# Two weight groups of a fused attention and MLP kernel loaded as one pair of 1024-column row blocks

## The chip, the cores and the metric

The kernel runs on one core of a Trainium2 chip. The metric is the device time of one launch in microseconds (us). A core has a matrix engine (TensorE, in profiles PE, with its weight loads as PEld), three engines for elementwise work (VectorE or DVE, ScalarE or ACT, GpSimd or POOL), and a queue engine (SyncE or SP) that issues most of the transfers between DRAM and the on-chip memory SBUF. Matmuls write to PSUM, which has eight banks here, PS0 to PS7, each 128 partitions by 512 float32.

## The reference

```python
def _attn_ref(q, k, v):                       # 8 batches, 8 heads, 576 tokens, 64 wide
    q_s = np.exp(q - np.max(q, axis=-1, keepdims=True))
    q_s = q_s / (np.sum(q_s, axis=-1, keepdims=True) + 1e-09)
    k_s = np.exp(k - np.max(k, axis=2, keepdims=True))
    k_s = k_s / (np.sum(k_s, axis=2, keepdims=True) + 1e-09)
    kv = np.einsum('bhsd,bhse->bhde', k_s, v)
    return np.einsum('bhsd,bhde->bhse', q_s, kv)

def _moe_ref(x, w_in, w_out, beta):           # x: 4608 x 512, w_in: 512 x 2048, w_out: 2048 x 512
    h = x @ w_in
    g = h * (1.0 / (1.0 + np.exp(-beta * h)))
    return g @ w_out
```

The attention result, with the heads side by side, is the x of the second function. Inputs and the output are float32.

## The kernel before

**Tiling.** The 4608 tokens are worked on in nine slabs of 512: the first 512 tokens of each of the eight batches, and a ninth slab of the 64 left over in each. A slab has a pass 1 (h for 16 tiles of 128 features, f = 0 to 15, each summed over four blocks m = 0 to 3 of the 512 inputs) and a pass 2 (four output tiles u = 0 to 3, each summed over the 16 features tiles). Between them ScalarE reads a finished h tile from its PSUM bank, applies the activation with beta, and writes it to GT in bfloat16 (L646). The attention of the next batch is mixed into the passes.

**Order.** The program is written out as one list of operations, each with its engine, the keys that it reads and writes, and the PSUM banks that it touches. The waits between engines are derived from that. Within an engine the order of the list is the order of execution; an instruction that waits holds up all that stand behind it on its engine. All transfers issued by SP move along one queue. In slab 0 the callbacks in the list `todo` put attention work of batch 1 between the matmuls of pass 2 at counted places.

**Weights.** w_in is loaded in float32 and cast to bfloat16 (`WIN`) in four groups c of 512 columns, that is, four feature tiles each: `load_win` (L565) issues the transfers, `cast_win` (L570, its instruction on L571) the casts. Each group has a staging buffer of [128, 4, 512] float32: WST0, WST1, and then the two output buffers O2S1 and O2S0, which are free at the start. Groups 0 to 2 come as four transfers of 256 KB (one block m each, rows of 2 KB), group 3 as two of 512 KB (two blocks m each, rows of 2 KB). After the casts, the same buffers take w_out (`load_wout`, L548), in pieces of 1 MB for f = 0 to 3, 4 to 7 and 8 to 11, then of 512 KB for 12 and 13, and of 256 KB each for 14 and 15. `scale_wout` (L558, its instruction on L560) multiplies each by 1/beta on VectorE and writes `WOUT` in bfloat16. Later O2S0 and O2S1 hold the finished output tiles for the stores.

**Slab 0.** `by_m(0, a, b)` gives a function that, for one m, runs the matmuls of tiles a to b - 1. The loop on L682 works through the groups of tiles 4 to 7, 8 to 11, 12 to 13 and 14 to 15, each over all four m. Which bank a tile of slab 0 uses is in `HFIRST` (L650): tiles 8 to 15 use banks 3, 4, 5, 6, 0, 1, 7, 2, and tiles 0 to 7 the same ones. Pass 2 of slab 0 writes its four outputs to banks 3, 4, 5 and 6, all four side by side for one f after the other:

```python
pass2_group(0, (0, 1, 2, 3), (3, 4, 5, 6), tick)
```

The work of batch 1 that stands around it in the list, before that call, is this. SP issues the loads for f = 0 and 4, the queries' first half, f = 8, the second half, then keys and values mixed with the remaining w_out loads. ScalarE takes the exponential of the queries (L312) after the last activation of pass 1, which needs a table load. `norm_main` then sums on VectorE (L336), takes the reciprocal there (L337) and multiplies on GpSimd (L338) for head pairs 0, 1, 3 and 2:

```python
scale_wout(0)
scale_wout(4)
exp_q(1, (0, 1, 3, 2))
norm_main(1, 0, 1, POOL)
scale_wout(8)
norm_main(1, 1, 1, POOL)
norm_main(1, 3, 1, POOL)
exp_kc(1, 0, 2)
scale_wout(12, 2)
cast_v(1, 1)
norm_main(1, 2, 1, POOL)
```

`scale_wout(14, 2)` and TensorE's transposes of the normalized queries of head pairs 0 and 1 (L368) follow as callbacks in pass 2.

Of the kernel before, what the change touches and what calls it, by code (L numbers as in the profile page):

```python
# [5 lines left out]
F32 = mybir.dt.float32  # L6
# [10 lines left out]
DM = H * D  # L17
DFF = 2048
NF = DFF // 128
NM = DM // 128  # L20
# [9 lines left out]
PE, ACTE, DVE, POOL, SP = "tensor", "scalar", "vector", "gpsimd", "sync"  # L30
# [13 lines left out]
class Program:  # L44
# [12 lines left out]
    def add(self, eng, fn, r=(), w=(), bank=(), slot=None, after=()):  # L57
        op = Op(eng, fn, slot)
        op.pos = len(self.ops)
        deps = op.deps  # L60
        deps.extend(after)
        for k in r:
            deps.extend(self.writer.get(k, ()))
            self.readers.setdefault(k, []).append(op)
        for k in w:
            for d in self.readers.get(k, ()):
                if d is not op and not self._same(d, op):
                    deps.append(d)
            for d in self.writer.get(k, ()):
                if not self._same(d, op):  # L70
                    deps.append(d)
            self.readers[k] = []
            self.writer[k] = [op]
        for k in bank:
            t = self.touch.setdefault(k, {})
            for e, d in t.items():
                if e != eng:
                    deps.append(d)
            t[eng] = op
        if eng == POOL and slot is None:  # L80
            if self.pool is not None:
                deps.append(self.pool)
            self.pool = op
        self.ops.append(op)
        return op
# [78 lines left out]
def bass_efficient_attn_shen__then__act_swish_beta_kernel(  # L164
# [10 lines left out]
    win_h, wout_h, beta_h, out_h = moe_w_in.tensor, moe_w_out.tensor, moe_beta.tensor, out.tensor  # L175

    with ExitStack() as es:
        def sb(name, shape, dt):
            return es.enter_context(nc.sbuf_tensor(name, shape, dt))
# [22 lines left out]
        WIN = sb("WIN", [128, NM, DFF], BF16)  # L202
        WST = [sb(f"WST{i}", [128, 4, DM], F32) for i in range(2)]
        WOUT = sb("WOUT", [128, NF, DM], BF16)
        GT = sb("GT", [128, NF, SM], BF16)
        O2S = [sb(f"O2S{i}", [128, 4, DM], F32) for i in range(2)]
        BT = sb("BT", [4, 512], F32)
        BC = sb("BC", [128, NF], F32)
        BETA = sb("BETA", [128, NF], F32)
        RB = sb("RB", [128, NF], F32)  # L210
# [12 lines left out]
        add = P.add  # L223
# [7 lines left out]
            r=["iota"], w=["idb"])  # L231
        add(POOL, lambda e: e.tensor_scalar(IDF[:, :], IOTA[0:4, 0:4], 0.0, None, ALU.is_equal),
            r=["iota"], w=["idf"])

        def homes_vk(i):
            add(POOL, lambda e: e.memset(VB[i][:, :, :, D:VW], 1.0), w=[("vone", i)])
# [52 lines left out]
        for hp in range(NHP):  # L289
            if hp % 2 == 0:  # L290
                add(SP, lambda e, hp=hp: e.dma_start(dst(QF[0], 2 * hp, 2), src(qt_h, 0, 2 * hp, 2)),  # L291
                    w=[("qf", 0, hp, hp // 2)], slot=f"qf0{hp}")
                continue
            for c in range(2):
# [3 lines left out]
                    w=[("qf", 0, hp, 2 + c)], slot=f"qf0{h}")  # L298
        add(ACTE, lambda e: e.dma_start(BT[:, :], bass.AP(beta_h, 0, [[512, 4], [1, 512]])),
            w=["bt"], slot="bt")  # L300
        for hp in range(NHP):
# [3 lines left out]
            w=["dummy"])  # L305
# [197 lines left out]
        def warm(n, bk, long=False):  # L503
            for _ in range(n):
                if long:
                    mm(PS[bk][:, :], bass.AP(XT8, 0, [[NM * SM, 128], [1, 256]]).bitcast(F32),
                       bass.AP(XT8, 0, [[NM * SM, 128], [1, 1024]]).bitcast(F32), True, True,
                       r=["xw"], w=[("ps", bk)], bk=bk)
                else:
                    mm(PS[bk][:, :], WARM[:, 0:128], WARM[:, :], True, True, r=["warm"],  # L510
                       w=[("ps", bk)], bk=bk)
# [27 lines left out]
        def go(steps):  # L539
            for s in steps:  # L540
                s()


        STAGE = (WST[0], WST[1], O2S[1], O2S[0])
        SKEY = [[(n, i, u) for u in range(4)]
                for n, i in (("wst", 0), ("wst", 1), ("o2", 1), ("o2", 0))]

        def load_wout(f, n=4):  # L548
            c, x = f // 4, f % 4
            if f < 8:  # L550
                a = bass.AP(wout_h, 512 * c * DM, [[2 * DM, 128], [256 * DM, 2], [1, 2 * DM]])
                o = bass.AP(STAGE[c], 0, [[4 * DM, 128], [2 * DM, 2], [1, 2 * DM]])
            else:
                a = bass.AP(wout_h, (512 * c + x) * DM, [[4 * DM, 128], [1, n * DM]])
                o = bass.AP(STAGE[c], x * DM, [[4 * DM, 128], [1, n * DM]])
            add(SP, lambda e: e.dma_start(o, a), w=SKEY[c][x:x + n], slot=f"wst{f}")

        def scale_wout(f, n=4):  # L558
# [6 lines left out]
        def load_win(c, m=0, nm=NM):  # L565
            a = bass.AP(win_h, m * 128 * DFF + 512 * c, [[DFF, 128], [128 * DFF, nm], [1, 512]])
            add(SP, lambda e: e.dma_start(STAGE[c][:, m:m + nm, :], a), w=SKEY[c][m:m + nm],  # L567
                slot=f"win{c}{m}")

        def cast_win(c, m, eng):  # L570
            add(eng, lambda e: e.tensor_copy(WIN[:, m, 512 * c:512 * c + 512], STAGE[c][:, m, :]),  # L571
                r=[SKEY[c][m]], w=[("win", c, m)])

        KB = 2

# [18 lines left out]

        homes_vk(0)
        homes_vk(1)
        for c in range(4):
            for m in range(0, NM, 1 if c < 3 else 2):
                load_win(c, m, 1 if c < 3 else 2)
        warm(3, 0, True)  # L600
        exp_q(0)
        for hp in range(NHP):
# [16 lines left out]
        for m in range(1, NM):  # L619
            cast_win(0, m, POOL)  # L620
        cast_win(1, 0, POOL)
        go(t_steps(0, (2,), (5,)))
        warm(1, 0)
# [4 lines left out]
        kv_tiles(2, 7)  # L628
        out_now(0, 1, 5, ACTE)
        cast_win(0, 0, DVE)  # L630
        warm(2, 3)
        out_now(0, 2, 0, ACTE)
# [4 lines left out]
        def pass1_mm(t, f, m, bk):  # L637
            x = XT8 if t == 8 else XT[t % 2]
            rd = ([("xt8", p_, y) for p_ in range(4) for y in range(2)] if t == 8
                  else [("xt", t % 2, m)])  # L640
            n = 2 if f < 8 else 4
            l = bass.AP(WIN, m * DFF + 128 * (f // n * n) + f % n, [[NM * DFF, 128], [n, 128]])
            mm(PS[bk][:, :], l, x[:, m, :], m == 0, m == NM - 1,
               r=rd + [("win", f // 4, m)], w=[("ps", bk)], bk=bk)
            if m == NM - 1:
                add(ACTE, lambda e: e.activation(GT[:, f, :], PS[bk][:, :], ACT.Silu,  # L646
                                                 scale=BETA[:, f:f + 1]),
                    r=[("ps", bk), "beta"], w=[("gt", f)], bank=[bk])
# [3 lines left out]
        def hbank(t, f):  # L652
            return HFIRST[t][f] if t < 2 and f < len(HFIRST[t]) else HB[f % 3]

        def by_m(t, a, b):
            def at(m, f0=a, f1=b):
                for f in range(f0, f1):
                    pass1_mm(t, f, m, hbank(t, f))
            return at

        def pass1_tile(t, f, tick):
# [6 lines left out]
        at = by_m(0, 0, 4)  # L668
# [5 lines left out]
            w=["dummy"])  # L674
        at(2)
        at(3)
        for c in range(1, 4):
            for m in range(1 if c == 1 else 0, NM):
                cast_win(c, m, DVE)
            if c == 1:  # L680
                add(DVE, lambda e: e.reciprocal(RB[:, :], BETA[:, :]), r=["beta"], w=["rb"])
        for g, n in ((4, 4), (8, 4), (12, 2), (14, 2)):  # L682
            at = by_m(0, g, g + n)
            for m in range(NM):
                at(m)
        load_wout(0)
        load_wout(4)
        load_swapped(1, (0, 2))
        load_wout(8)
        load_swapped(1, (3, 1))  # L690
        load_k(1, 4, (0, 1))
# [8 lines left out]
        def o2_evac(t, u, bk, eng=DVE):  # L700
            add(eng, lambda e: (e.copy if eng == ACTE else e.tensor_copy)(  # L701
                O2S[t % 2][:, u, :], PS[bk][:, :]),
                r=[("ps", bk)], w=[("o2", t % 2, u)], bank=[bk])

        def store(t):
            a = bass.AP(out_h, t * S * DM, [[4 * DM, 128], [1, 4 * DM]])
            add(SP, lambda e: e.dma_start(a, O2S[t % 2][:, :, :]),
                r=[("o2", t % 2, u) for u in range(4)], slot=f"out{t % 2}")

        def store8(u, c0=0, c1=DM, key=None):  # L710
            for h in range(2):
                a = bass.AP(out_h, ((2 * u + h) * S + SM) * DM + c0, [[DM, 64], [1, c1 - c0]])
                add(SP if h == 0 else ACTE,
                    lambda e, h=h, a=a: e.dma_start(a, O2S[0][64 * h:64 * h + 64, u, c0:c1]),
                    r=[key or ("o2", 0, u)], slot=f"outr{u}{h}{c0}")

        def last_tile(u, parts, bks):
            for (c0, c1), bk in zip(parts, bks):
                for f in range(NF):
                    mm(PS[bk][:, 0:c1 - c0], GT[:, f, 128 * u:128 * u + 128], WOUT[:, f, c0:c1],  # L720
                       f == 0, f == NF - 1, r=[("gt", f), ("wout", f)], w=[("ps", bk)], bk=bk)
                add(DVE, lambda e, c0=c0, c1=c1, bk=bk: e.tensor_copy(  # L722
                    O2S[0][:, u, c0:c1], PS[bk][:, 0:c1 - c0]),
                    r=[("ps", bk), ("o2", 0, u)], w=[("o2c", c0)], bank=[bk])
# [20 lines left out]
        for t in range(NSLAB):  # L745
# [17 lines left out]
            slot = [0]  # L763
# [30 lines left out]
            if t == 0:  # L794
# [16 lines left out]
                while todo:  # L811
                    todo.pop()[1]()
                at = by_m(1, 0, FIRST[1])
# [3 lines left out]
                    r=["warm"], w=["dummy"])  # L817
# [81 lines left out]
```

## Time and profile before

| | |
|---|---|
| Median of four runs | 279.42 us (279.27 to 280.52) |
| The profiled execution | 279.35 us, of which the span from the first to the last instruction is 277.6 us |
| TensorE busy | 272.8 us, 98% of the span |
| ScalarE busy | 165.6 us, 60% |
| VectorE busy | 102.2 us, 37% |
| GpSimd busy | 34.3 us, 12% |
| Granted TensorE clock | 1.00 in every stretch from 13 us on |
| Busy share of the transfer engines, 13 to 42 us | 0.98 to 1.05 |
| Rate of the transfers, 13 to 42 us | 361 to 401 GB/s by stretch |

The profile is of one execution. Busy time is the time in which an engine works on an instruction; times of day are counted in us from the start of the span. A row of a timeline names the start, the duration, the engine, the line of the code, the operation, what is written and read (written<-read), the shape and the number of instructions taken together, and in brackets how long the engine was idle before and what ended the wait. The chain that ended last is followed back from the last instruction: at each step to what released it, or to the instruction before it on its engine. A share above 1 in the transfer engines' busy time comes from packets that overlap.

### The profile page before, as it was taken

Reading aid. Unit: us, or ns where it says so; the run is one execution under the profiler, and the core shown is the slowest. Engines: PE = TensorE matmul, PEld = TensorE weight load, DVE = VectorE, ACT = ScalarE, POOL = GpSimd, SP = SyncE. Lnnn points to the kernel's source line nnn. Section 1 sums busy time; section 2 is a strip of 40 time slices with the busy share of each in tenths; the row PEclk is TensorE's granted clock in tenths of the full one; section 3 lists DMA queues with packets and bytes.
Section 4 is the critical chain, followed back from the end, with each engine's and each line's share of the span. In section 5 each row is a group of like instructions: output and inputs, shape, how many; then the busy total and the mean of one; then the engine's idle time right before and its main releaser. Section 6 shows DMA issues by size and latency. Waiting matters only on the chain.

```text
span 277.6 us, 4649 instructions
## 1 busy us (share of the span) xinstructions
PE 272.8 (98%) x1937; PEld 132.0 (48%) x1937; DVE 102.2 (37%) x205; ACT 165.6 (60%) x239; POOL 34.3 (12%) x52
## 2 busy tenths in 40 slices
PE   7999999999999999999999999999999999999995
PEld 3545444444445444545454545454444444444444
DVE  4754685017660149115820564036503200110012
ACT  5858466999478747783579447953741275027500
POOL 2630151036200301230003000000000000000000
PEclk9999999999999999999999999999999999999999
DMA  7999998999199499991699134002500110011022
GB/s 243 370 392 403 386 387 256 353 392 271 40 322 341 93 302 407 386 149 31 185 386 178 32 152 94 2 4 113 132 0 2 76 76 2 0 81 70 2 76 76
DMA packets 43421, 50.38 MB, mean 182 GB/s; under 512 B 22148, under 2 KB 30724, under 8 KB 42248
## 3 DMA queue, kind: packets, MB, share of 16 engines
q1 hardware_dynamic: 42480, 49.16, 54.8%
q10 hardware_dynamic: 920, 0.93, 1.1%
q8 instruction: 15, 0.25, 0.4%
q14 instruction: 6, 0.05, 0.0%
HBM read 36.71 MB, written 9.44 MB: 166 GB/s over the span
## 4 chain that ended last, share of the span: by engine, by line
PE 84%; DMA 10%; SPq 3%; DVE 1%; issue 0%
PE PS L370 84%; DMA WST<-in_moe_w_out_dram 4%; DMA O2S<-in_moe_w_out_dram 4%; DMA WST<-in_moe_w_in_dram 3%; SPq L250 1%; SPq L567 1%; DVE WOUT L560 1%; SPq L291 0%; SPq L296 0%; DVE WIN L571 0%; DVE O2S L722 0%; SPq L147 0%
## 5 line engine op out<-in xcount | busy, mean ns | idle before, releaser
L646 ACT ACTIVATE GT<-PS,BETA 128x512 bf16<-128x512 f32 x144 | 96.5, 691 | 61.4 <-PE PS L370 61.4
L370 PE MATMUL PS<-WOUT,GT 128*128 128x512 bf16 (+2 forms) x608 | 127.9, 368 | 0.1
L370 PE MATMUL PS<-XT,WIN 128*128 128x512 bf16 x576 | 126.4, 379 | 0.1
L370 PEld LDWEIGHTS PS<-XT,WIN 128*128 128x128 bf16 x576 | 60.5, 106 | 63.7 <-issue 0.5
L370 PEld LDWEIGHTS PS<-WOUT,GT 128*128 128x128 bf16 x608 | 57.3, 98 | 65.8 <-issue 1.0
L701 DVE COPY O2S<-PS 128x512 f32<-128x512 f32 x33 | 22.6, 688 | 124.5 <-PE PS L370 124.5
L355 POOL CAST VB<-VF 128x576 bf16<-128x576 f32 x29 | 19.7, 679 | 88.2 <-DMA VF<-in_v_dram 86.9
L336 DVE TENSOR_REDUCE QS<-EQ 128x8 f32<-128x512 bf16 (+1 forms) x22 | 20.1, 912 | 17.3 <-ACT EQ L312 17.3
L320 ACT ACTIVATE EK<-KF 128x1152 bf16<-128x1152 f32 (+1 forms) x19 | 18.5, 1006 | 3.0 <-DMA KF<-in_k_dram 2.8
L457 ACT CAST XT<-PS 128x512 bf16<-128x512 f32 x14 | 7.6, 587 | 21.0 <-PE PS L370 21.0
L312 ACT ACTIVATE EQ<-QF 128x512 bf16<-128x512 f32 x32 | 17.6, 616 | 3.8 <-DMA QF<-in_q_dram 3.8
L338 DVE TENSOR_TENSOR EQ<-EQ,QI 128x1024 bf16<-128x1024 bf16 (+1 forms) x12 | 13.9, 1160 | 0.4
L338 POOL TENSOR_TENSOR EQ<-EQ,QI 128x512 bf16<-128x512 bf16 x10 | 10.6, 1063 | 27.1 <-DVE QI L337 26.7
L457 DVE CAST XT<-PS 128x512 bf16<-128x512 f32 x14 | 9.1, 687 | 12.2 <-PE PS L370 12.2
L370 PEld LDWEIGHTS PS<-VB,EK 64*64 64x64 bf16 x576 | 6.7, 107 | 4.2 <-issue 2.6
L370 PE MATMUL PS<-VB,EK 64*64 64x65 bf16 x576 | 8.0, 194 | 0.2 <-POOL VB L355 0.2
L646 ACT ACT_TABLE_LOAD x5 | 6.4, 1283 | 0.1
L370 PE MATMUL PS<-XT 128*128 128x512 f32 x6 | 4.9, 985 | 1.5 <-DVE XT L226 1.5
L370 PE MATMUL PS<-QT,KVC 64*64 64x512 bf16 x64 | 6.3, 384 | 0.0
L560 DVE TENSOR_SCALAR WOUT<-O2S,RB 128x512 bf16<-128x512 f32 x8 | 4.5, 602 | 2.6 <-DMA O2S<-in_moe_w_out_dram 2.6
L337 DVE RECIPROCAL QI<-QS 128x8 f32<-128x8 f32 (+1 forms) x22 | 5.0, 226 | 0.8
L320 ACT ACT_TABLE_LOAD x4 | 5.1, 1283 | 0.1
(51 smaller groups left out, 67.0 us busy)
## 6 DMA issues: line engine op xcount, KB each, us to landing
out_dram<-O2S SPq DMA_DIRECT2D x8, 1024.0 KB, 4.6
QF<-in_q_dram SPq DMA_DIRECT2D x30, 256.0 KB, 5.7
KF<-in_k_dram SPq DMA_DIRECT2D x6, 1152.0 KB, 8.3
VF<-in_v_dram SPq DMA_DIRECT2D x6, 1152.0 KB, 11.0
KF<-in_k_dram SPq DMA_DIRECT2D x8, 288.0 KB, 7.9
VF<-in_v_dram SPq DMA_DIRECT2D x8, 288.0 KB, 8.2
WST<-in_moe_w_in_dram SPq DMA_DIRECT2D x8, 256.0 KB, 7.5
WST<-in_moe_w_out_dram SPq DMA_DIRECT2D x2, 1024.0 KB, 10.5
```

Source lines behind the costliest of these rows:

```text
L250: add(engs[c % len(engs)], lambda e, a=a, o=o: e.dma_start(o, a), w=[(name, i, hp) for hp in range(c * n, c * n + n)], slot=f"{name}{i}_{c}")
L312: add(ACTE, lambda e, o=o, a=a: e.activation(o, a, ACT.Exp), r=[("qf", i, hp, x) for x in ((2, 3) if hp % 2 else (hp // 2,))], w=[("eq", i ...
L320: add(ACTE, lambda e: e.activation(o, a, ACT.Exp), r=[("kf", i, h) for h in range(hp, hp + n)], w=[("ekc", i, h) for h in range(hp, hp + n)])
L336: add(DVE, lambda e: e.tensor_reduce(s_, a, AX.X, ALU.add), r=ks, w=[("qs", i, hp0)])
L337: add(DVE, lambda e: e.reciprocal(v_, s_), r=[("qs", i, hp0)], w=[("qi", i, hp0)])
L338: add(eng, lambda e: e.tensor_tensor(a, a, vb, ALU.mult), r=ks + [("qi", i, hp0)], w=ks)
L355: add(eng, lambda e: (e.copy if eng == ACTE else e.tensor_copy)(o, a), r=[("vf", i, hp), ("vone", i)], w=[("vb", i, hp, h) for h in ((0, 1 ...
L370: add(PE, lambda e: e.matmul(o, l, r_, start=start, stop=stop, tile_position=tp), r=r, w=w, bank=[bk])
L457: add(eng, lambda e, eng=eng, bk=bk, hp=hp: (e.copy if eng == ACTE else e.tensor_copy)(XT[i][:, hp, :], PS[bk][:, :]), r=[("ps", bk)], w=[ ...
L560: add(DVE, lambda e, f=f: e.tensor_scalar(WOUT[:, f, :], STAGE[f // 4][:, f % 4, :], RB[:, f:f + 1], None, ALU.mult), r=[SKEY[f // 4][f % ...
L646: add(ACTE, lambda e: e.activation(GT[:, f, :], PS[bk][:, :], ACT.Silu, scale=BETA[:, f:f + 1]), r=[("ps", bk), "beta"], w=[("gt", f)], ba ...
L701: add(eng, lambda e: (e.copy if eng == ACTE else e.tensor_copy)(O2S[t % 2][:, u, :], PS[bk][:, :]), r=[("ps", bk)], w=[("o2", t % 2, u)], ...
```

## The change

Groups 2 and 3 of w_in are loaded together: for each block m one transfer of 512 KB whose rows are 1024 columns, 4 KB, long. The two output buffers become the halves of one buffer O2 of [128, 8, 512], with O2S1 as the first and O2S0 as the second half. Pair m lies in units 2m and 2m + 1 of it. The loads of w_out for f from 8 on go to the same places of O2 as before. VectorE casts the pairs in the order in which they come, group 2 and then group 3 for each m. TensorE works on tiles 8 to 15 as one group: tiles 8 to 13 for m = 0 and 1, tiles 14 and 15 for m = 0 and 1, and then all eight for m = 2 and for m = 3.

```diff
@@ -203,7 +203,8 @@
         WST = [sb(f"WST{i}", [128, 4, DM], F32) for i in range(2)]
         WOUT = sb("WOUT", [128, NF, DM], BF16)
         GT = sb("GT", [128, NF, SM], BF16)
-        O2S = [sb(f"O2S{i}", [128, 4, DM], F32) for i in range(2)]
+        O2 = sb("O2", [128, 8, DM], F32)
+        O2S = (O2[:, 4:8, :], O2[:, 0:4, :])
         BT = sb("BT", [4, 512], F32)
         BC = sb("BC", [128, NF], F32)
         BETA = sb("BETA", [128, NF], F32)
@@ -544,6 +545,7 @@
         STAGE = (WST[0], WST[1], O2S[1], O2S[0])
         SKEY = [[(n, i, u) for u in range(4)]
                 for n, i in (("wst", 0), ("wst", 1), ("o2", 1), ("o2", 0))]
+        PAIR = SKEY[2] + SKEY[3]
 
         def load_wout(f, n=4):
             c, x = f // 4, f % 4
@@ -552,7 +554,7 @@
                 o = bass.AP(STAGE[c], 0, [[4 * DM, 128], [2 * DM, 2], [1, 2 * DM]])
             else:
                 a = bass.AP(wout_h, (512 * c + x) * DM, [[4 * DM, 128], [1, n * DM]])
-                o = bass.AP(STAGE[c], x * DM, [[4 * DM, 128], [1, n * DM]])
+                o = bass.AP(O2, (f - 8) * DM, [[8 * DM, 128], [1, n * DM]])
             add(SP, lambda e: e.dma_start(o, a), w=SKEY[c][x:x + n], slot=f"wst{f}")
 
         def scale_wout(f, n=4):
@@ -567,9 +569,18 @@
             add(SP, lambda e: e.dma_start(STAGE[c][:, m:m + nm, :], a), w=SKEY[c][m:m + nm],
                 slot=f"win{c}{m}")
 
+        def load_pair(m):
+            a = bass.AP(win_h, m * 128 * DFF + 1024, [[DFF, 128], [1, 2 * DM]])
+            o = bass.AP(O2, 2 * m * DM, [[8 * DM, 128], [1, 2 * DM]])
+            add(SP, lambda e: e.dma_start(o, a), w=PAIR[2 * m:2 * m + 2], slot=f"winp{m}")
+
         def cast_win(c, m, eng):
-            add(eng, lambda e: e.tensor_copy(WIN[:, m, 512 * c:512 * c + 512], STAGE[c][:, m, :]),
-                r=[SKEY[c][m]], w=[("win", c, m)])
+            if c < 2:
+                s_, key = STAGE[c][:, m, :], SKEY[c][m]
+            else:
+                s_, key = O2[:, 2 * m + c - 2, :], PAIR[2 * m + c - 2]
+            add(eng, lambda e: e.tensor_copy(WIN[:, m, 512 * c:512 * c + 512], s_),
+                r=[key], w=[("win", c, m)])
 
         KB = 2
 
@@ -594,9 +605,11 @@
 
         homes_vk(0)
         homes_vk(1)
-        for c in range(4):
-            for m in range(0, NM, 1 if c < 3 else 2):
-                load_win(c, m, 1 if c < 3 else 2)
+        for c in range(2):
+            for m in range(NM):
+                load_win(c, m, 1)
+        for m in range(NM):
+            load_pair(m)
         warm(3, 0, True)
         exp_q(0)
         for hp in range(NHP):
@@ -674,15 +687,21 @@
             w=["dummy"])
         at(2)
         at(3)
-        for c in range(1, 4):
-            for m in range(1 if c == 1 else 0, NM):
+        for m in range(1, NM):
+            cast_win(1, m, DVE)
+        add(DVE, lambda e: e.reciprocal(RB[:, :], BETA[:, :]), r=["beta"], w=["rb"])
+        for m in range(NM):
+            for c in (2, 3):
                 cast_win(c, m, DVE)
-            if c == 1:
-                add(DVE, lambda e: e.reciprocal(RB[:, :], BETA[:, :]), r=["beta"], w=["rb"])
-        for g, n in ((4, 4), (8, 4), (12, 2), (14, 2)):
-            at = by_m(0, g, g + n)
-            for m in range(NM):
-                at(m)
+        at = by_m(0, 4, 8)
+        for m in range(NM):
+            at(m)
+        at = by_m(0, 8, NF)
+        for a, b in ((8, 14), (14, NF)):
+            for m in range(2):
+                at(m, a, b)
+        at(2)
+        at(3)
         load_wout(0)
         load_wout(4)
         load_swapped(1, (0, 2))
```

## The prediction

> **What bounds the kernel now.** I first read the page's busy shares: TensorE (PE) works 272.8 of 277.6 us, so only what makes PE wait can cost or gain time. Then the chain that ended last, in order of time (start us, us, what). Before 41.81 it runs through weight loads, after it through matmuls alone:
>
> ```profile
> 30.89 9.84 DMA O2S<-in_moe_w_out_dram
> ...
> 40.75 1.01 DVE WOUT L560
> ...
> 41.81 232.86 PE PS L370 x1641
> ```
>
> So the stretch that the change touches (w_in groups 3 and 4, 21 to 28 us) lies before a point that a later load sets. How much cover is that? PE's timeline answers (start us, us, instructions x count):
>
> ```profile
> 15.01 13.12 PE L370 MATMUL PS<-XT,WIN 128*128 128x512 bf16 x60
> 27.97 9.88 PE L370 MATMUL PS<-WOUT,GT 128*128 128x512 bf16 x45
> 37.68 0.61 PE L368 MATMUL PS<-IDB,EQ 128*128 128x128 bf16 x8
> 38.13 2.23 PE L370 MATMUL PS<-WOUT,GT 128*128 128x512 bf16 x9
> 40.29 0.48 PE L370 MATMUL PS<-VB,EK 64*64 64x65 bf16 x36
> 40.70 1.71 PE L370 MATMUL PS<-WOUT,GT 128*128 128x512 bf16 x6
> 42.34 0.53 PE L370 MATMUL PS<-QT,KVC 64*64 64x512 bf16 x4
> ```
>
> 60 matmuls from 15.01 to 27.97 are 0.216 us each: no stall in pass 1. The nine from 38.13 to 40.29 take 2.16, against 9 x 0.216 = 1.94 and about 0.10 for the change of tile shape (five take 1.18 from 44.95 to the next such change, so 0.10): 0.12 of waiting. The six from 40.70 to 42.34 take 1.64 against 1.30 + 0.10: 0.24. Both are waits for a scaled WOUT tile (f = 12 and f = 15). **The cover is only about 0.35 us**: a PE delay before 38 us beyond that reaches the end, and no gain can exceed about 0.35.
>
> ScalarE's timeline shows who empties the PSUM banks:
>
> ```profile
> 24.07 3.58 ACT L646 ACTIVATE GT<-PS,BETA 128x512 bf16<-128x512 f32 x6 [1.03 <-PE PS L370]
> 27.95 1.27 ACT L646 ACTIVATE GT<-PS,BETA 128x512 bf16<-128x512 f32 x2 [0.30 <-PE PS L370]
> 29.24 1.28 ACT L312 ACT_TABLE_LOAD   x1
> 30.53 0.63 ACT L312 ACTIVATE EQ<-QF 128x512 bf16<-128x512 f32 x1
> ```
>
> Six take 3.58 with one lasting 0.69: pitch (3.58 - 0.69)/5 = 0.58 us, against 0.216 for PE. It keeps up because tiles f = 8..11 finish four to five us before pass 2. VectorE (DVE) and GpSimd (POOL) show loads and the chain behind ScalarE:
>
> ```profile
> 21.76 0.43 DVE L571 CAST WIN<-O2S 128x512 bf16<-128x512 f32 x1 [0.25 <-DMA O2S<-in_moe_w_in_dram]
> 23.11 0.76 DVE L571 CAST WIN<-O2S 128x512 bf16<-128x512 f32 x2 [0.92 <-DMA O2S<-in_moe_w_in_dram]
> 24.46 0.76 DVE L571 CAST WIN<-O2S 128x512 bf16<-128x512 f32 x2 [0.59 <-DMA O2S<-in_moe_w_in_dram]
> ...
> 33.74 1.68 DVE L560 TENSOR_SCALAR WOUT<-O2S,RB 128x512 bf16<-128x512 f32 x4 [1.53 <-DMA O2S<-in_moe_w_out_dram]
> ...
> 37.89 1.34 DVE L560 TENSOR_SCALAR WOUT<-O2S,RB 128x512 bf16<-128x512 f32 x2 [0.86 <-DMA O2S<-in_moe_w_out_dram]
> ...
> 40.75 1.00 DVE L560 TENSOR_SCALAR WOUT<-O2S,RB 128x512 bf16<-128x512 f32 x1 [0.19 <-DMA O2S<-in_moe_w_out_dram]
> ```
>
> ```profile
> 36.39 2.16 POOL L338 TENSOR_TENSOR EQ<-EQ,QI 128x512 bf16<-128x512 bf16 x2 [3.06 <-DVE QI L337]
> ...
> 40.21 1.25 POOL L338 TENSOR_TENSOR EQ<-EQ,QI 128x512 bf16<-128x512 bf16 x1
> ```
>
> A scale costs 0.42 in a group of four, but 1.00 at 40.75, while POOL's multiply (40.21 to 41.46) runs; and that multiply takes 1.25 rather than about 1.05 because a scale stood before it.
>
> **The change part by part.**
>
> *Loads.* Six transfers (four of 256 KB, two of 512 KB, 2 KB rows) become four of 512 KB with 4 KB rows; SP issues two fewer (about 0.47 us each), but it waits afterwards anyway: its first w_out load is issued only at 16.10, after POOL's cast. Bytes are the same. Landings now: 512 KB in 1.35 us (23.11 to 24.46). With 4 KB rows the first two w_out megabytes' scales begin 27.01 and 29.70, that is 2.55 and 2.69 us after what landed before, so 1.28 to 1.35 per 512 KB. Gain on four pairs: 0 to 0.3, I take 0.15, on every later landing. The Trainium skill's page "DMA: Bandwidth & Descriptors", section "Anatomy of one DMA — SWDGE (gpsimd) path", fits a fixed 2.0 us per DMA (measured for another issuing engine); two transfers fewer would by that be worth 4 us. The trace disagrees: queued 256 KB loads land 0.68 apart (casts at 21.08 and 21.76), at 388 GB/s, fixed parts overlapped. I use the row. Even this gain can show only through the 0.35 above.
>
> *Casts.* The same eight of 0.43 us, other order. Pairs 0 and 1 land where the second and fourth 256 KB landed, about 20.38 and 21.74. PE starts f = 8 at 21.06, m = 1 at 22.36 (+6 x 0.216). The casts needed end 20.83 and 22.19: in time, with slack cut to about 0.2 (it was 0.5 or more). For m = 2 (24.51) and m = 3 (26.24) slack is 1.0 or more. Taken as nothing; a landing 0.5 late would cost 0.3. DVE has only these casts then.
>
> *Waits of SP.* The f = 8 w_out load needs the first half of O2, now freed by both casts of pair 1: at about 22.55 rather than 22.21. Behind it on SP's queue stand two QF loads, two K loads, the f = 12 load and V loads. The data queue is backlogged (the loads issued at 16.1 and 19.6 land at 27 and 29.7), so 0.35 costs nothing unless the backlog, about 9 us, is gone. The f = 12 load is released at about 23.9 as before and issued at 27.16 anyway.
>
> *The group of eight.* Same 32 matmuls, so PE still ends pass 1 at 27.97. Banks for f = 12..15 at m = 0 come from f = 4..7: needed 21.92, 22.14, 23.65, 23.87; ScalarE empties them at 21.3, 21.9, 22.5, 23.03. No wait. But f = 8..15 now all finish in the last 1.73 us. First activation: the m = 3 matmul of f = 8 at 26.24, plus 0.42 (23.65 to 24.07 today) = 26.66. Ends: f = 8 27.35, f = 9 27.93, f = 10 28.51, f = 11 29.08, f = 15 31.38. Pass 2 writes its four outputs into just those banks (3 to 6) at 27.97, 28.18, 28.40, 28.62. The fourth waits for 29.08 + 0.05: **0.52 us of PE stall**. That operation isn't in the trace: bounds are 0 (were the banks free earlier) and 0.8 (pitch 0.65).
>
> *The chain behind ScalarE.* It is free at 31.38, not 29.22: table load to 32.68, exp of head pair 0 to 33.32 (31.16 now), DVE's reduction and reciprocal to 34.28. DVE's scales f = 8..11 queue behind: they start 34.2 rather than 33.74, before PE needs them (35.4). But POOL's multiply for head pair 0 moves from 32.29 to about 34.4, onto those scales. Who goes first? The trace has POOL arriving 0.13 after a scale started (40.21) and held 0.2, that is one scale. The page "SBUF — State Buffer", section "Who interferes with whom", says that such a pair shares ports and the first to issue locks out the other for its whole instruction: a rule against this change. By it POOL enters after one scale: 34.55 to 35.6, and the scales end at 36.67 (three more). Were DVE to keep the port, they end at 35.9. Then head pair 1: reduction and reciprocal to 37.5, POOL to 38.6. PE's transposes of it come at 37.90 + 0.52 = 38.42: **0.24 more** by the rule, 0 if DVE keeps the port. I take 0.24.
>
> *f = 12..15.* Head pair 3's multiply runs to about 39.8. Scale 13 either slips in before it (39.3) or after it (40.15); head pair 2's multiply then begins about 41.05 or 41.25. Scale 15 is then done either before it (41.3), or, if its turn comes just after, at about 42.55, where PE needs it at 41.46 + 0.76 = 42.22. So 0 to 0.4; I take 0.1, since scale 15 has landed by 40.7 in the likelier order. KVC and V work behind moves along with PE.
>
> Sum: 0.52 + 0.24 + 0.10 - 0.35 = **+0.5 us**. The profiled execution took 279.35 (span 277.6, 1.75 around it), 0.07 under the median 279.42: so 279.9, and a span of about 278.1. A measurement of this kernel can tell about 0.3%, 0.84 us.
>
> **Rivals.**
> 1. *The shared port turns on the last scale.* If scale 13 comes after head pair 3's multiply, head pair 2's multiply holds scale 15 to 42.55: 0.52 + 0.24 + 0.4 - 0.35 = +0.8, and up to +1.3 if the reductions slip too: 280.2 to 280.7. It decides once that multiply starts before scale 15 and ends after 41.9. For: the 1.00 row. Against: scale 15 has 0.3 to 0.5 us of free port before. 33%.
> 2. *DVE keeps the port through its four scales*: only the bank wait is left, 0.52 - 0.35 = +0.17: 279.6. For: scales follow each other at 0.40. Against: the 40.21 row. 12%.
> 3. *The bank wait is small and loads are earlier*: both w_out waits shrink, -0.2 to -0.35: 279.1 to 279.2. 5%. Were 4 us per the fixed-cost rule true, the PE would still cap it at -0.35.
> 4. *The rows are still moved in 2 KB pieces*: then the 0.15 is zero; no change to the sum, since the stalls decide. Inside the cases above.
>
> **How the numbers follow.** The sum's own case, +0.2 to +0.8, has 50%. Slower by over 0.84: most of rival 1 (0.30) and a tail of the main case (0.05): 0.35. Faster by over 0.84: the cap forbids it but for something unseen, 0.03. Within: 0.62. The range from 279.2 to 280.8 leaves out rival 3's low end and rival 1's high end.
>
> **What would show it.** PE: a gap of about 0.5 within the first four matmuls of pass 2, waiting on ScalarE; ScalarE: one run of eight activations from about 26.7 to 31.4 (or 8 with no idle between), table load at 31.4; POOL's first multiply of that batch near 34.4 rather than 32.29; scales f = 8..11 stretched to over 2 us; the last piece of the chain beginning at 42.0 to 42.6 rather than 41.81. It is wrong if PE starts pass 2 after 28.1 (then the w_in loads or casts were late), if pass 2 starts with no gap, or if the chain's last PE piece begins before 41.8.

## The result and the profile after

The changed kernel takes 280.21 us (median of 37 runs, 279.83 to 281.87) against 279.64 us for the kernel before in the same sessions (58 runs). The ratio is 1.0023 with a 95% interval of 1.0015 to 1.0031, that is +0.64 us (0.42 to 0.87). The loss is real, and below the 0.84 us that the prediction set as its bound for "slower". A second series gave 280.25 us against 279.65, ratio 1.0019 (1.0006 to 1.0032). The profiled execution is one of the longer ones: 280.83 us, with a span of 279.0.

Lines of the code have moved a little: the activation is now on L659, scales on L562, casts on L582, GpSimd's multiply on L339, matmuls on L371. In the changed kernel the joined buffer is named O.

First TensorE's timeline after (start us, us, what, how many):

```profile
15.34 13.12 PE L371 MATMUL PS<-XT,WIN 128*128 128x512 bf16 x60
28.30 0.98 PE L371 MATMUL PS<-WOUT,GT 128*128 128x512 bf16 x3
29.47 9.24 PE L371 MATMUL PS<-WOUT,GT 128*128 128x512 bf16 x42 [0.19 <-ACT GT L659]
38.55 0.88 PE L369 MATMUL PS<-IDB,EQ 128*128 128x128 bf16 x8
39.26 2.10 PE L371 MATMUL PS<-WOUT,GT 128*128 128x512 bf16 x9
41.30 0.48 PE L371 MATMUL PS<-VB,EK 64*64 64x65 bf16 x36
41.71 1.75 PE L371 MATMUL PS<-WOUT,GT 128*128 128x512 bf16 x6
43.39 0.54 PE L371 MATMUL PS<-QT,KVC 64*64 64x512 bf16 x4
43.86 1.04 PE L371 MATMUL PS<-WOUT,GT 128*128 128x512 bf16 x4
```

Read starts, not ends: a row's end overlaps the start of the next one. Pass 1 is still 60 matmuls without a stall: 15.34 to 28.30 is 12.96 us, as before. In pass 2 three matmuls take 3 x 0.216 = 0.65, but the fourth comes at 29.47: 0.52 us of waiting, and the releaser is ScalarE's activation. The transposes start at 38.55 and are followed at 39.26, 0.71 later, where it was 0.45: 0.26 of waiting. The nine matmuls to 41.30 take 2.04, just 9 x 0.216 + 0.10: the old wait for f = 12 is gone, used up as cover. The six from 41.71 to 43.39 take 1.68 against 1.40: 0.28 of waiting for f = 15, which was 0.24. In all 0.52 + 0.26 + 0.28 - 0.12 - 0.24 = 0.70 us.

One wait stands in both profiles and cancels, and the prediction did not count it. Further rows of the kernel before:

```profile
42.81 1.04 PE L370 MATMUL PS<-WOUT,GT 128*128 128x512 bf16 x4
...
46.13 0.41 PE L370 MATMUL PS<-QT,KVC 64*64 64x512 bf16 x4
46.47 1.90 PE L370 MATMUL PS<-XT,WIN 128*128 128x512 bf16 x8
```

Four products with KVC take 0.34 to the next matmul when nothing holds them up (46.13 to 46.47), but 0.47 at 42.34, and 0.47 again at 43.39 in the changed kernel. KVC is made on VectorE behind the held scale of f = 15. So the cover in the kernel before was 0.35 + 0.13 = 0.48 us, and the changed kernel pays the 0.13 as before.

Pass 1 starts 0.33 later here. It starts at 15.01, 14.85 and 15.65 in the three profiles with the old loads, and between 15.21 and 15.47 in the ten with the new ones, so no difference can be told from that. Behind 43.86 nothing systematic is left: from the matmul after the KVC products to the end of the span it is 234.8 us before, 235.1 here and 234.6 in the profile of experiment 1.

ScalarE after, and the chain of work that ended last, followed back from 50 us:

```profile
26.99 4.74 ACT L659 ACTIVATE GT<-PS,BETA 128x512 bf16<-128x512 f32 x8 [3.62 <-PE PS L371]
31.75 1.28 ACT L313 ACT_TABLE_LOAD   x1
33.04 0.63 ACT L313 ACTIVATE EQ<-QF 128x512 bf16<-128x512 f32 x1
```

```profile
26.99 4.74 ACT GT L659 x8
...
34.63 2.33 DVE WOUT L562 x4
...
38.57 1.86 DVE WOUT L562 x2
...
41.27 1.54 DVE WOUT L562 x2
...
42.86 7.35 PE PS L371 x69
```

Eight activations run as one block of 4.74 us, after 3.62 us with nothing to do: the same work as before, pushed together at the end. The chain before 42.86 no longer consists of weight loads. It is ScalarE's backlog, and then VectorE.

VectorE and GpSimd after:

```profile
23.01 0.76 DVE L582 CAST WIN<-O 128x512 bf16<-128x512 f32 x2 [0.51 <-DMA O<-in_moe_w_in_dram]
24.30 0.76 DVE L582 CAST WIN<-O 128x512 bf16<-128x512 f32 x2 [0.53 <-DMA O<-in_moe_w_in_dram]
...
34.54 2.41 DVE L562 TENSOR_SCALAR WOUT<-O,RB 128x512 bf16<-128x512 f32 x4
...
38.49 1.94 DVE L562 TENSOR_SCALAR WOUT<-O,RB 128x512 bf16<-128x512 f32 x2
...
41.18 1.62 DVE L562 TENSOR_SCALAR WOUT<-O,RB 128x512 bf16<-128x512 f32 x2
```

```profile
34.71 1.17 POOL L339 TENSOR_TENSOR EQ<-EQ,QI 128x512 bf16<-128x512 bf16 x1 [17.59 <-DVE QI L338]
37.93 2.22 POOL L339 TENSOR_TENSOR EQ<-EQ,QI 128x512 bf16<-128x512 bf16 x2 [2.05 <-DVE QI L338]
...
41.41 1.11 POOL L339 TENSOR_TENSOR EQ<-EQ,QI 128x512 bf16<-128x512 bf16 x1 [0.46 <-DVE QI L338]
```

The loads did get faster: pairs are cast every 1.28 us (23.01, 24.30), where 512 KB took 1.35. But the scales now meet GpSimd's multiplies at worse moments. In the kernel before, head pair 0's multiply was done before the four scales began at 33.74:

```profile
32.29 1.04 POOL L338 TENSOR_TENSOR EQ<-EQ,QI 128x512 bf16<-128x512 bf16 x1 [15.46 <-DVE QI L337]
```

Now the four take 2.41 instead of 1.68. The two for f = 12 and 13 met one multiply before (1.34) and meet two now (1.94). The last scale, of f = 15, was held by a multiply before (1.00) and is held again (1.62 for the last two), but it ends at 42.80 instead of 41.75.

### The profile page after: what moved, and what is told of

It is laid out like the page before. It is cut to its first block, busy times and chain, and to the rows that moved or that the text cites. A ratio compares the mean times of both kernels' runs of the same rounds, so it can differ in the third digit from the quotient of the medians.

```text
span 279.0 us, 4647 instructions
## 1 busy us (share of the span) xinstructions
PE 273.2 (98%) x1937; PEld 131.9 (47%) x1937; DVE 103.1 (37%) x205; ACT 165.6 (59%) x239; POOL 35.2 (13%) x52
## 4 chain that ended last, share of the span: by engine, by line
PE 88%; DVE 3%; ACT 3%; DMA 3%; SPq 1%; issue 0%
PE PS L371 88%; DMA KF<-in_k_dram 3%; DVE WOUT L562 2%; ACT GT L659 2%; SPq L251 1%; DVE QS L337 1%; ACT L313 0%; SPq L292 0%; DVE QI L338 0%; ACT EK L321 0%; ACT EQ L313 0%; ACT XT L536 0%; SPq L297 0%; DVE O L741 0%
## 5 line engine op out<-in xcount | busy, mean ns | idle before, releaser
L659 ACT ACTIVATE GT<-PS,BETA 128x512 bf16<-128x512 f32 x144 | 96.4, 691 | 63.7 <-PE PS L371 63.6
L371 PE MATMUL PS<-WOUT,GT 128*128 128x512 bf16 (+2 forms) x608 | 128.1, 368 | 0.3 <-ACT GT L659 0.2
L371 PE MATMUL PS<-XT,WIN 128*128 128x512 bf16 x576 | 126.3, 379 | 0.0
L371 PEld LDWEIGHTS PS<-XT,WIN 128*128 128x128 bf16 x576 | 60.5, 106 | 63.5 <-issue 0.5
L371 PEld LDWEIGHTS PS<-WOUT,GT 128*128 128x128 bf16 x608 | 57.3, 98 | 66.2 <-issue 1.0
L720 DVE COPY O<-PS 128x512 f32<-128x512 f32 x33 | 22.6, 688 | 124.6 <-PE PS L371 124.6
L356 POOL CAST VB<-VF 128x576 bf16<-128x576 f32 x29 | 20.6, 710 | 88.3 <-DMA VF<-in_v_dram 86.8
L339 POOL TENSOR_TENSOR EQ<-EQ,QI 128x512 bf16<-128x512 bf16 x10 | 10.7, 1067 | 27.8 <-DVE QI L338 27.4
L339 DVE TENSOR_TENSOR EQ<-EQ,QI 128x1024 bf16<-128x1024 bf16 (+1 forms) x12 | 13.9, 1159 | 0.4
L371 PEld LDWEIGHTS PS<-VB,EK 64*64 64x64 bf16 x576 | 6.7, 107 | 4.9 <-issue 2.8
L371 PE MATMUL PS<-VB,EK 64*64 64x65 bf16 x576 | 8.0, 194 | 0.8 <-ACT VB L356 0.4
L371 PE MATMUL PS<-QT,KVC 64*64 64x512 bf16 x64 | 6.3, 385 | 0.3 <-issue 0.3
L371 PE MATMUL PS<-XT 128*128 128x512 f32 x6 | 4.6, 940 | 1.5 <-DVE XT L227 1.5
L562 DVE TENSOR_SCALAR WOUT<-O,RB 128x512 bf16<-128x512 f32 x8 | 6.0, 798 | 0.0
```

Source lines behind the costliest of these rows:

```text
L339: add(eng, lambda e: e.tensor_tensor(a, a, vb, ALU.mult), r=ks + [("qi", i, hp0)], w=ks)
L371: add(PE, lambda e: e.matmul(o, l, r_, start=start, stop=stop, tile_position=tp), r=r, w=w, bank=[bk])
L562: add(DVE, lambda e, f=f: e.tensor_scalar(WOUT[:, f, :], STAGE[f // 4][:, f % 4, :], RB[:, f:f + 1], None, ALU.mult), r=[SKEY[f // 4][f % ...
```

## The experiments

All ratios are to runs of the kernel before on the same chip. In most of these traces one record of a run of matmuls is missing, so that x59, x44, x41 and x5 stand for 60, 45, 42 and 6.

**1. The changed kernel again.** No edit.

> The changed kernel once more, as the yardstick for the runs beside it. Theory P (the stalls of the prediction: fourth output bank waiting for ScalarE 0.52 us, transposes waiting for GpSimd's multiply 0.25, last scaled w_out tile 0.25 to 0.4, less the 0.35 of cover): +0.5 to +0.8 us over the kernel before. Rival L (the loads or casts of w_in are late and pass 1 stalls): TensorE shows gaps between the first matmul of tile 8 and the start of pass 2. Rival C (something else in the program, such as where instructions are fetched): the gaps lie after 50 us.

280.25 us, 1.0019 (1.0006 to 1.0032). The same waits stand in its trace, in the same places (fourth matmul of pass 2, transposes, last scale). Pass 1 takes 12.96 us again (15.38 to 28.34), with nothing late: rival L is out for the changed kernel as it ran here. So is rival C, since the rest of the span is no longer than before.

**2. Finish in two groups of four.**

```diff
-        at(2)
-        at(3)
+        for a, b in ((8, 12), (12, NF)):
+            for m in (2, 3):
+                at(m, a, b)
```

> New loads, but the last two blocks m are run for tiles 8 to 11 first and then for tiles 12 to 15, so that ScalarE starts on tile 8 about 0.87 us earlier. Theory P: no gap at the start of pass 2 (bank 6 free at about 28.2 counted as in the kernel before, needed at 28.6), ScalarE done near 30.5 instead of 31.4; the wait of the transposes shrinks to about 0.15, the one for the last scale stays at 0.2 to 0.3. In all +0.1 to +0.2 us over the kernel before, so about 0.5 faster than the changed kernel. Rival L: the loads are as in the changed kernel, so the time stays at +0.5 to +0.8.

279.69 us, 1.0000 (0.9989 to 1.0010). With the loads untouched the loss is gone, within an interval (-0.3 to +0.3 us) that also holds the +0.1 to +0.2 that was expected. TensorE's timeline:

```profile
21.82 7.07 PE L371 MATMUL PS<-XT,WIN 128*128 128x512 bf16 x31 [0.26 <-DVE WIN L582]
28.72 9.90 PE L371 MATMUL PS<-WOUT,GT 128*128 128x512 bf16 x44
38.46 0.79 PE L369 MATMUL PS<-IDB,EQ 128*128 128x128 bf16 x8
39.09 2.10 PE L371 MATMUL PS<-WOUT,GT 128*128 128x512 bf16 x9
```

Pass 2 starts with 44 matmuls in one row, no gap. The transposes take 0.63 to the next matmul: 0.18 of waiting is left. The wait for f = 15 is left as well (0.29). The first row shows something else. In this one execution the loads came some 0.8 us later (the last pair was cast at 25.08, not 24.30), and pass 1 waited for a cast: it took 13.38 us (15.34 to 28.72) instead of 12.96. So the cut in slack has a price in executions where the loads run late. It is the only one of the nine profiles with these loads and this order of m = 0 and 1 that shows it; how often it happens was not measured.

**3. The late finish with the old loads.**

```diff
-        for g, n in ((4, 4), (8, 4), (12, 2), (14, 2)):
-            at = by_m(0, g, g + n)
-            for m in range(NM):
-                at(m)
+        at = by_m(0, 4, 8)
+        for m in range(NM):
+            at(m)
+        at = by_m(0, 8, NF)
+        for a, b in ((8, 12), (12, NF)):
+            for m in range(3):
+                at(m, a, b)
+        at(3)
```

> The kernel before with its own loads and casts, but tiles 8 to 15 run their last block m together: tiles 8 to 11 for m = 0 to 2, tiles 12 to 15 for m = 0 to 2, then all eight for m = 3. Theory P: the finishing order alone makes the loss: a gap of about 0.5 us in the first four matmuls of pass 2, the transposes' wait of about 0.25, +0.5 to +0.8 us over the kernel before. Rival L: with the old loads the loss is gone, 0 to +0.1.

280.36 us, 1.0031 (1.0018 to 1.0045). The loss is there in full (+0.71 us by the medians, +0.87 by the ratio), so neither the joined buffer nor the 4 KB rows are needed for it. The same signature in TensorE's and ScalarE's timelines:

```profile
28.61 0.98 PE L370 MATMUL PS<-WOUT,GT 128*128 128x512 bf16 x3
29.78 9.24 PE L370 MATMUL PS<-WOUT,GT 128*128 128x512 bf16 x41 [0.19 <-ACT GT L646]
```

```profile
27.30 4.74 ACT L646 ACTIVATE GT<-PS,BETA 128x512 bf16<-128x512 f32 x8 [3.62 <-PE PS L370]
```

29.78 - 28.61 - 0.65 = 0.52 us again, and again a block of eight activations of 4.74.

**4. The loads alone.** Loads and casts of the changed kernel, with the loop over groups of 4, 4, 2 and 2 tiles of the kernel before put back.

> The new loads and casts alone: TensorE works through tiles 4 to 7, 8 to 11, 12 and 13, 14 and 15 as in the kernel before. Theory P with the page of loads: tile 8 needs pair 2 at 22.8 and pair 3 at 23.7 (plus 0.3 for a start as late as in the two profiles of the changed kernel), casts end at about 23.45 and 24.75, so pass 1 stalls by 0.8 to 1.1 us in two places; no bank gap at the start of pass 2, no wait of the transposes, and the two waits for scaled w_out tiles vanish: +0.45 to +0.8 us over the kernel before. Rival: the data come early enough, and the time is that of the kernel before (-0.2 to +0.1).

279.88 us, 1.0004 (0.9995 to 1.0013). TensorE's timeline:

```profile
15.21 9.08 PE L371 MATMUL PS<-XT,WIN 128*128 128x512 bf16 x40
24.53 4.51 PE L371 MATMUL PS<-XT,WIN 128*128 128x512 bf16 x19 [0.23 <-DVE WIN L582]
28.87 9.88 PE L371 MATMUL PS<-WOUT,GT 128*128 128x512 bf16 x44
```

From 15.21 to 28.87 is 13.66 us for 60 matmuls, 0.70 more than 12.96, most of it in two waits for casts (at 23.24 and 24.53). Expected were 0.8 to 1.1. In this execution pair 2 was cast at 22.75, where the changed kernel's profile had 23.01, so the data were a quarter of a microsecond earlier. Less the 0.48 of cover this makes +0.22; measured is +0.1 (-0.15 to +0.36), below the 0.45 to 0.8 that was expected. So in this execution, with pairs loaded together, the old order also waits for data. The new order removes that wait and pays with ScalarE's.

**5. A group of six, then two.** As experiment 2, with `((8, 14), (14, NF))`.

> New loads; the last two blocks m are run for tiles 8 to 13 first and then for tiles 14 and 15, so six tiles finish close together and ScalarE starts on tile 8 about 0.43 us earlier than in the changed kernel (halfway between it and the version that finishes in two groups of four). Theory P (the loss grows with how far ScalarE is behind at the end of pass 1): gap at the start of pass 2 about 0.1 instead of 0.52, transposes 0 to 0.1, last scale about 0.2; +0.05 to +0.25 us over the kernel before. Rival T (a threshold: any new order costs the same): +0.5 to +0.7.

279.78 us, 1.0002 (0.9993 to 1.0012): at the low end of what was expected. The trace has a wait of 0.09 in the first four matmuls of pass 2, 0.26 at the transposes and 0.28 at the last scale: 0.63 - 0.35 = +0.28 by this one execution. The gap at the start of pass 2 thus goes 0.52, 0.09, 0 for eight, six and four tiles that finish together. The wait of the transposes was expected to be 0 to 0.1: the 0.43 us that ScalarE gained did not bring the transposes' wait down, since TensorE too arrived 0.43 earlier.

**6. No multiply for head pair 0.** The multiply of `norm_main(1, 0, ...)` is left out.

> The changed kernel without GpSimd's multiply of head pair 0 of batch 1 (its queries are not normalized: this part of the computation is left out). Theory P with the port shared by VectorE and GpSimd: the four scales f = 8 to 11 go back from 2.4 to 1.7 us, head pair 1 follows 0.7 earlier, the transposes no longer wait (0.25 saved); the bank wait of 0.5 stays, the last scale's wait falls to 0 to 0.2; +0.15 to +0.4 us over the kernel before. Rival without a shared port (the four scales are slow for another reason, such as their reading from the joined buffer): the scales stay at 2.4 us and the time at +0.5 to +0.8.

279.75 us, 1.0005 (0.9995 to 1.0015). VectorE's and TensorE's timelines:

```profile
34.42 1.62 DVE L564 TENSOR_SCALAR WOUT<-O,RB 128x512 bf16<-128x512 f32 x4
```

```profile
38.42 0.61 PE L371 MATMUL PS<-IDB,EQ 128*128 128x128 bf16 x8
38.87 2.10 PE L373 MATMUL PS<-WOUT,GT 128*128 128x512 bf16 x9
```

The four scales are at 1.62 again, from the same joined buffer. The slow scales come from the multiply beside them. The transposes take 0.45, no wait; neither is there one for f = 15. The KVC products take 0.34 to the next matmul. What remains is the bank gap of 0.52 less the cover of 0.48: +0.04, against +0.1 measured (-0.15 to +0.4).

**7. Scales ahead of the normalization.**

```diff
-                norm_main(1, 0, 1, POOL)
                 scale_wout(8)
+                norm_main(1, 0, 1, POOL)
```

> The changed kernel with the scales of f = 8 to 11 put ahead of head pair 0's normalization on VectorE. Theory P: the bank gap of 0.52 stays; the four scales start with their landing (33.5) and take 1.7 us, since GpSimd's multiply now comes after them (about 36); the transposes don't wait, and the last scale is done when TensorE comes to it: 0 to 0.1. In all 0.52 - 0.35, that is +0.1 to +0.3 us over the kernel before. Rival Q (the 0.25 at the transposes comes from ScalarE's late exponential itself, not from the order of scales and multiply): transposes still wait 0.2 to 0.3 and the time is +0.5 to +0.8.

279.76 us, 0.9999 (0.9989 to 1.0010). Nothing is left out here. VectorE's and TensorE's timelines:

```profile
33.34 1.68 DVE L562 TENSOR_SCALAR WOUT<-O,RB 128x512 bf16<-128x512 f32 x4 [2.27 <-DMA O<-in_moe_w_out_dram]
```

```profile
28.30 0.98 PE L371 MATMUL PS<-WOUT,GT 128*128 128x512 bf16 x3
29.47 9.24 PE L371 MATMUL PS<-WOUT,GT 128*128 128x512 bf16 x41 [0.19 <-ACT GT L659]
38.54 0.61 PE L369 MATMUL PS<-IDB,EQ 128*128 128x128 bf16 x8
38.99 2.11 PE L371 MATMUL PS<-WOUT,GT 128*128 128x512 bf16 x9
...
42.84 0.41 PE L371 MATMUL PS<-QT,KVC 64*64 64x512 bf16 x4
43.18 1.04 PE L371 MATMUL PS<-WOUT,GT 128*128 128x512 bf16 x4
```

ScalarE's block of eight activations starts at 26.99, and so its exponential is as late as in the changed kernel, and the gap of 0.52 stands. Yet the transposes no longer wait: the order of scales and multiply made that 0.26, not the late exponential itself. Rival Q is out. The wait for f = 15 and the one for KVC (0.34 from 42.84 to 43.18) are gone too, since everything behind on VectorE comes earlier. The gap of 0.52 less 0.48 of cover is +0.04: the bank wait alone is nearly all hidden, which the expectation of +0.1 to +0.3 had a little too high.

**8. Head pair 2's multiply after the last scale.**

```diff
-                norm_main(1, 2, 1, POOL)
-                t_dma(1, 2, 2)
-                load(2)
+                norm_main(1, 2, 1, None)
...
-                        (111.1, lambda: scale_wout(14, 2)), (119.1, ...
+                        (111.1, lambda: scale_wout(14, 2)),
+                        (111.2, lambda: (late_mul[0](DVE), t_dma(1, 2, 2), load(2))), (119.1, ...
```

With `None`, `norm_main` gives the sum and the reciprocal only; `late_mul` holds the multiply for later.

> The changed kernel with only head pair 2's multiply moved to VectorE, after the scale of f = 15. Theory P (the three waits add up): the wait for the last scale (0.28 in the profile of the changed kernel) goes, the bank wait of 0.52 and the transposes' 0.25 stay: 0.52 + 0.25 - 0.35, that is +0.3 to +0.5 us over the kernel before. Rival S (the waits hide one another, and the last one would not matter, or the time falls to that of the kernel before): outside of that, +0.6 or more, or 0.

280.06 us, 1.0016 (1.0008 to 1.0025): +0.45 us, within the expectation. In VectorE's timeline the two last scales are at half their time:

```profile
41.10 0.83 DVE L569 TENSOR_SCALAR WOUT<-O,RB 128x512 bf16<-128x512 f32 x2
```

The wait for f = 15 is gone from TensorE and the 0.52 at the start of pass 2 stays, as do the transposes' 0.26. So the three waits add up in the trace; the medians alone, whose intervals overlap the changed kernel's, would not show it. A tenth comes back: the moved multiply holds up the KVC work on VectorE, and the four products with KVC take 0.57 to the next matmul, where the changed kernel has 0.47.

**9. A version without the waits.** Experiment 2's order, head pair 0's multiply on VectorE in its place, and experiment 8's edit. It was timed in two series.

> New loads, last two blocks m in two groups of four tiles, and two multiplies taken off GpSimd: head pair 0's runs on VectorE in its place, head pair 2's on VectorE after the scale of f = 15 (with the transposing transfer and the loads of batch 2 behind it). Theory P: no bank gap, no wait of the transposes, the last scale takes 0.5 us and isn't waited for; only the wait for f = 12 (0.1) is left: -0.1 to -0.3 us against the kernel before, if the later loads of batch 2 cost nothing. Rival: what is freed is lost again behind the head pair 2 multiply (KVC on VectorE about 0.3 later, query transpose about 0.3 later): 0 to +0.4.

> The version with new loads, groups of four at the end and the free port once more, beside the kernel before with the free port: -0.2 to -0.4 us against the kernel before. Theory P: no difference from that one beyond 0.1. Rival L: 0.15 or more ahead of it.

The first series gave 279.37 us, 0.9987 (0.9980 to 0.9995), ahead of both kernels, where a gain of 0.1 to 0.3 us was expected. The second gave 279.69 us, 1.0001 (0.9990 to 1.0011), where 0.2 to 0.4 was expected. In both traces the waits at the start of pass 2, at the transposes, for f = 12 and for f = 15 are gone. TensorE in the first:

```profile
28.28 9.88 PE L378 MATMUL PS<-WOUT,GT 128*128 128x512 bf16 x44
37.99 0.61 PE L376 MATMUL PS<-IDB,EQ 128*128 128x128 bf16 x8
38.44 2.10 PE L378 MATMUL PS<-WOUT,GT 128*128 128x512 bf16 x9
```

From pass 1's first matmul to the one after the KVC products both traces take 27.40 us (15.31 to 42.71, 15.47 to 42.87), against 27.80 before (15.01 to 42.81). Yet that it beats the kernel before is not settled: one series says 0.1% and one says nothing. Both ratios are below the changed kernel's 1.0023 (1.0015 to 1.0031).

**10. The kernel before with those multiplies moved.** Its own loads and groups.

> The kernel before, with its own loads and groups, and only the two multiplies taken off GpSimd as in the version with the free port (head pair 0's on VectorE in its place, head pair 2's on VectorE after the scale of f = 15). Theory P (the loads give nothing that reaches the end): the wait for f = 15 (0.23) goes, the one for f = 12 (0.12) may stay: -0.2 to -0.35 us against the kernel before, the same as the version with the new loads within the interval. Rival L (the 4 KB rows give the gain): 0 to -0.05, clearly less than with the new loads.

279.64 us, 1.0002 (0.9994 to 1.0010): no gain, where 0.2 to 0.35 was expected. Its trace shows no wait for f = 15, but 0.52 us at f = 12, whose weights came later in that execution; VectorE's and TensorE's timelines:

```profile
38.27 1.20 DVE L567 TENSOR_SCALAR WOUT<-O2S,RB 128x512 bf16<-128x512 f32 x2 [0.93 <-DMA O2S<-in_moe_w_out_dram]
```

```profile
37.97 0.81 PE L377 MATMUL PS<-WOUT,GT 128*128 128x512 bf16 x3
39.14 1.47 PE L377 MATMUL PS<-WOUT,GT 128*128 128x512 bf16 x6 [0.35 <-DVE WOUT L567]
...
42.71 0.65 PE L377 MATMUL PS<-QT,KVC 64*64 64x512 bf16 x4 [0.29 <-DVE RC L446]
43.28 1.04 PE L377 MATMUL PS<-WOUT,GT 128*128 128x512 bf16 x4
```

The landing moved by 0.4 (37.89 in the profile of before), as much as the whole gain at stake. And TensorE now waits for KVC ahead of its four products, since the moved multiply stands before that work on VectorE: what the edit freed is lost again behind it, which was the rival of experiment 9. Beside experiment 9's second series (1.0001) there is no difference that could be put down to the 4 KB rows. Whether they give anything at the end stays open at the size of 0.1%.

## Why the prediction was right, point by point

- **The cover of 0.35.** The trace shows it spent: the wait for f = 12 is gone, and the one for f = 15 is back. It was read 0.13 too small, since the KVC products also waited. That left the sum as it was, because the changed kernel has this wait too. But "no gain can exceed about 0.35" was too strict, and where only the bank wait is left (experiments 6 and 7), the traces leave +0.04 of it and not the 0.17 of the second rival.
- **The bank wait, 0.52.** Measured 0.52 in the changed kernel and 0.52 with the old loads. The pitch of 0.58 us was right within 2%: eight in 4.74 make (4.74 - 0.69)/7 = 0.58.
- **The transposes, 0.24.** Measured 0.26. The prediction had chosen between GpSimd entering after one scale and VectorE keeping the port (0). For the first it had the nearest row, and the rule of the Trainium skill's page "SBUF — State Buffer", section "Who interferes with whom", that the first to issue holds the shared ports for its whole instruction. GpSimd entered: its multiply ran 34.71 to 35.88 and the four scales took 2.41, 0.73 more than in the clear. Experiments 6 and 7 show it by taking the multiply away and by moving the scales ahead.
- **The last scale, 0 to 0.4, taken as 0.1.** This term was mis-sized: it measured 0.28. The step that failed is "scale 13 either slips in before it or after it", where the first was held likelier. The two scales took 1.94, so scale 13 did come after head pair 3's multiply: scale 12, held by the multiply before that, ended only at 39.25, when this one (39.05 to 40.15) was already running. And head pair 2's multiply (41.41 to 42.52) then held the last scale to 42.80. This is the mechanism of the first rival, which had 33%, with two thirds of its price. Experiment 8 takes it away.
- **The sum.** 0.52 + 0.26 + 0.28 - 0.36 = 0.70 by the trace, +0.64 by the runs, +0.5 predicted: right in direction and place, 0.14 to 0.2 short, nearly all of it in the last term. It was partly luck that the sum came so close: on f = 15 the less likely course happened, and only its low price kept the time beside the main case. The 280.21 us lie where the main case's +0.2 to +0.8 ends and the first rival's 280.2 to 280.7 begins.
- **The loads.** 0.15 was taken out of 0 to 0.3; 4 x (1.35 - 1.28) = 0.28 was measured. As predicted, it reaches no end: after 28 us TensorE waits for engines, not for loads. The 4 us that a fixed cost per transfer would have promised are nowhere.
- **The casts.** They were in time in both profiles of the changed kernel, but the slack of 0.2 was not put to the test there. The first cast of the pairs ended at 20.89, and tile 8 came at 15.34 + 28 x 0.216 = 21.39: 0.5 of slack, since pass 1 had started later. In the one execution of experiment 2 it did not suffice.
- **Where pass 2 starts.** The prediction called itself wrong if that came after 28.1; it came at 28.30. That sign was badly chosen: pass 1 had also started 0.33 later, and only its length (12.96 us, unchanged) tells whether w_in was late. Likewise the last piece of the chain begins at 42.86, outside of the forecast 42.0 to 42.6, and at 42.53 once the 0.33 is taken off.

## What to carry to other kernels

A matrix engine can keep its pace through a regrouping and still lose. Count what the engine that drains its banks has left to do when the last group ends: eight tiles at 0.58 us behind a matrix engine at 0.216, with the next stage in the very same banks, cost half a microsecond at once and as much again down the line. Before a reordering for larger loads, ask whether loads set the pace at that point. Finishing the tiles in two halves kept the new loads and took the loss away.

## What the runs showed of the hardware

A VectorE scale that meets a GpSimd multiply is recorded as long as the wait lasts (1.00 instead of 0.48), and ends about 0.29 us after the multiply does (41.46 and 41.75 in the kernel before, 42.52 and 42.80 in the changed one). A multiply that comes during a run of scales gets in after the first one here: it arrived at 34.71, the second scale began at 34.89 and lasted 1.27 us, to 0.28 after the multiply's end at 35.88. And the landing of a given load differs between executions with the same loads by 0.4 to 0.8 us (37.89 and 38.27 for f = 12 in experiment 10, 24.30 and 25.08 for the last pair in experiment 2), as much as the effects studied here, so that one execution's waits are no measure of a median.
